# Fewer, longer weight loads, a reordered W2 and one unevenly spread load of keys in a two-layer decode kernel

## The chip, the cores and the metric

The kernel runs on one core of a Trainium2 chip. Its time is the device time of one execution in microseconds; the time shown is the median of several executions. A profile is one more execution, traced by the hardware: all durations in this document come from such traces. A core has five engines (TensorE or PE, VectorE or DVE, ScalarE or ACT, GpSimd or POOL, SyncE or SP), each with its own instruction stream, and 16 DMA engines that move data between DRAM and the core's memory of 128 partitions. SP and ACT issue the transfers here, each in its own queue; all transfers of both queues run on the same 16 DMA engines. A transfer tells by a semaphore that it has landed.

## The reference

One token goes twice through attention with a key/value cache and an MLP, with a residual around each and a normalization ahead of each:

```python
x = A_x                                            # 1 x 1 x 640
x = x + _A_ref(_layernorm(x), k_cache, v_cache, wq, wo)
x = x + _B_ref(_layernorm(x), w1, w2)
x = x + _A_ref(_layernorm(x), k_cache, v_cache, wq, wo)
x = x + _B_ref(_layernorm(x), w1, w2)
```

`_A_ref` makes 32 queries of 128 from x (wq is 640 x 4096), scores each against its head's 8192 keys, takes a softmax, sums the head's 8192 values by it, and multiplies the 32 results by wo (4096 x 640). `_B_ref` is x times w1 (640 x 1728), a ReLU, and times w2 (1728 x 640). All is float32. Keys and values are 268 MB and are needed in both layers, so nearly all of them are loaded twice.

## The kernel before

Keys and values lie in DRAM in units, one contiguous block a unit, with 128 rows, one row a partition (`UNITS`, `ORDER`, lines 41 to 82). Most units are 6 MB (48 KB a partition) and hold parts of two heads; heads 0 to 3 and 28 to 31 have smaller ones (4 MB, 2 MB and less). Units are loaded into `ring`, a tile of 133 KB a partition that a first-fit search fills (`place`, line 158). `pump` (line 177) issues the next unit's load from SP as soon as a place is free; `release` (line 231) gives a place back when PE has read it, and pumps again. Layer 0 goes through the heads from 0 to 31; layer 1 takes 31 to 24 first, of which some units are kept in the ring, and ends with 3, 2, 1, 0 (`HEADS`, line 83).

For each head PE makes the scores (`scores`, line 484, matmul at L489), DVE and ACT the softmax, PE the sum of the values (`values`, L540), and DVE and PE reduce it to a column (`output`, L557 to L581). Work that belongs to no single head runs between the pieces of a head, as chores taken in order from two lists (`due`, line 713; `work_off`, line 667; `side_work`, line 738):

- Heads are taken in eight runs of four (`HG` = 4, `NG` = 8). At the first head of a run, `run_out` (line 682) multiplies the last run's four results by wo (`projected`, L458), and then has ACT load the part of wo of the next run: `load_wo` (line 259) loads 128 x 2560 floats, 1280 KB, into `wo_t`.
- At the third head of a run, `queries_of` (line 676) makes the next run's queries from the run's part of wq (`wide_queries`, line 411, matmul at L416), and then has ACT load the part for the run after it: `load_wq` (line 254), also 128 x 2560 floats, into `wq_t`.

Each of the two tiles has a single buffer, so a load waits until PE has read what stood there. The first part of wq and of wo are loaded at the start from SP, and a run's wq at the start of layer 1 by a call of its own.

W2 lies in DRAM as 128 rows of 14 blocks of 640 floats. The blocks are loaded by SP in parts, 0 to 4 and 4 to 8 in `pump` (L199) once the last unit of a layer is issued, and 8 to 10, 10 to 12, 12 and 13 by `more_of_w2` (line 208, L210); a part takes its columns of every row, so that its rows lie 14 x 640 floats apart in DRAM. In layer 0 some of them are issued within `mlp` (line 815), after PE has read the tile that they go to.

The order of the loads in the queues is that of the program, per issuing engine. The program gives loads a semaphore out of eight in turn; a load whose semaphore is still in use waits on its issuing engine for the earlier landing.

Of the kernel before, what the change touches and what calls it, by code (L numbers as in the profile page):

```python
# [10 lines left out]
F32 = mybir.dt.float32  # L11
# [69 lines left out]
    ]  # L81
ORDER = [(h, i) for h in range(H) for i in range(len(UNITS[h]))]
HEADS = [list(range(H)), [*range(31, 23, -1), *range(12, 24), *range(4, 12), 3, 2, 1, 0]]
KEPT = [(29, 0), (29, 1), (29, 6)]
BY_WO = KEPT[0]
BESIDE = 4
# [3 lines left out]
FLAT = 3072  # L90
EDGE = 4096
BIG = 1536


def wide(kind, piece):
# [18 lines left out]


@with_exitstack
def decode_kernel(ctx: ExitStack, tc: tile.TileContext, x, kv, wq, wo, w1, w2, out):
    nc = tc.nc
    consts = ctx.enter_context(tc.tile_pool(name="consts", bufs=1))
    wts = ctx.enter_context(tc.tile_pool(name="wts", bufs=1))  # L120
# [56 lines left out]
    def pump():  # L177
        while todo:
            layer, u = todo[0]
            n = size(u)  # L180
            at = place(layer, u, n)
            if at is None:
                return
            todo.pop(0)
            o = dram_at[u]
            nc.sync.dma_start(
                ring[:, 8 * at : 8 * (at + n)],
                kv[o : o + 8 * P * n].rearrange("(p m) -> p m", p=P),
            )
            for t, (_, kind, piece) in enumerate(UNITS[u[0]][u[1]]):  # L190
                m = wide(kind, piece)
                live[layer, u, t] = at, m
                at_of[layer, u, t] = ring, 8 * at
                at += m
            if not todo or layer < todo[0][0]:
                assert all(a + m <= RING for a, m in live.values())
                live["w2"] = RING, W2_UNITS
                for a, b in W2_PARTS[:: 1 - 2 * layer]:
                    nc.sync.dma_start(w2_t[:, a:b], w2[:, a:b])  # L199
        n = (FB - SLOTS) * D // 8  # L200
        if not w2_rest:
            at = place(1, (0, None), n)
            if at is not None:
                w2_rest.append(ring[:, 8 * at : 8 * (at + n)].rearrange("p (b d) -> p b d", d=D))
                for a, b in W2_MORE:
                    more_of_w2(a, b, w2_rest[0][:, a - SLOTS : b - SLOTS])

    def more_of_w2(a, b, where):
        rows = W2_LAST if a == FB - 1 else P
        nc.sync.dma_start(where[:rows], w2[:rows, a:b])  # L210

    def load_into(u, where, queue):
        n = 8 * size(u)
# [35 lines left out]
                if (of, its) == (h, kind):  # L249
                    yield piece, (L, (owner, i), t)  # L250

    wq_t, wo_t = {}, {}

    def load_wq(g, queue):
        t = wts.tile([P, NB * HG * DH], F32, name="wq_t")
        wq_t[g] = t.rearrange("p (c n) -> p c n", c=NB)
        queue.dma_start(t, wq[P * g : P * g + P])

    def load_wo(L, g, queue):

        wo_t[g] = wts.tile([P, HG, D], F32, name="wo_t")
        first, end = (L and g == 0), HG - (not L and g == NG - 1)
        if end < HG:
            load_into(BY_WO, wo_t[g][:, end], queue)
            at_of[0, BY_WO, 0] = wo_t[g][:, end], 0
        queue.dma_start(wo_t[g][:, first:end], wo[g][:, first:end])

    def wo_of(L, h):
        return wo_last if h == H - 1 or (L and h == 0) else wo_t[h // HG][:, h % HG]

    xr = work.tile([P, DR], F32, name="xr", bufs=2)
    load_wq(0, nc.sync)
# [116 lines left out]
    def queries(g, xc, r):  # L389

        pq = ps_m.tile([P, 512], F32, name="px")
        for c in range(NB):
            for j in range(HG):
                nc.tensor.matmul(
                    pq[32 * j : 32 * j + 32, :DH],
                    xc[:, c : c + 1].to_broadcast([P, 32]),
                    wq_t[g][:, c, j * DH : (j + 1) * DH],
                    start=(c == 0),
                    stop=(c == NB - 1),
                )  # L400
        yield "dve"
        row = work.tile([P, DR], F32, name="q_row")[:, :DH]
        nc.vector.tensor_scalar(row, pq[:, :DH], r[0], SCALE, op0=ALU.mult, op1=ALU.mult)
        yield "pe"
        pt = ps_m.tile([P, 512], F32, name="px")
        nc.tensor.matmul(pt[:, :HG], row, sel[:, :HG], start=True, stop=True)
        yield "dve"
        qT[g] = work.tile([P, HG], F32, name="qT", bufs=2)
        nc.vector.tensor_copy(qT[g], pt[:, :HG])

    def wide_queries(g, xc, r):

        pq = ps_m.tile([P, 512], F32, name="px")
        for c in range(NB):
            strip = c % 4
            nc.tensor.matmul(  # L416
                pq[32 * strip : 32 * strip + 32],
                xc[:, c : c + 1].to_broadcast([P, 32]),
                wq_t[g][:, c],
                start=c < 4,  # L420
                stop=c in (1, 2, 3, 4),
                skip_group_check=True,
            )
        for j in range(HG):
            yield "dve"
            row = work.tile([P, DR], F32, name="q_row")[:, :DH]
            mine = pq[:, j * DH : (j + 1) * DH]
            nc.vector.tensor_scalar(row, mine, r[0], SCALE, op0=ALU.mult, op1=ALU.mult)  # L428
            yield "pe"
            nc.tensor.matmul(  # L430
                mine[:, :1], row, one_of_each, start=True, stop=True, skip_group_check=True
            )
        yield "dve"
        qT[g] = work.tile([P, HG], F32, name="qT", bufs=2)
        nc.vector.tensor_copy(qT[g], pq.rearrange("p (j d) -> p j d", d=DH)[:, :, 0])

    def centre_query(g, j):

        mine = wq_t[g][:, :, j * DH : (j + 1) * DH]
        pq = ps_m.tile([P, 512], F32, name="px")  # L440
        for c in range(NB):
            nc.tensor.matmul(
                pq[:, :DH],
                ones.to_broadcast([P, P]),
                mine[:, c],
                start=c == 0,
                stop=c == NB - 1,
            )
        yield "dve"
        for c in range(NB):  # L450
            nc.vector.scalar_tensor_tensor(
                mine[:, c], pq[:, :DH], -1.0 / D, mine[:, c], op0=ALU.mult, op1=ALU.add
            )
# [195 lines left out]
    def attention_and_mlp(L, xr, s, before=None):  # L649
# [1 line left out]
        heads = HEADS[L]  # L651
        last = heads[-1]
        runs = [heads[a : a + HG] for a in range(0, H, HG)]
        groups = [run[0] // HG for run in runs]
        runs[-1] = runs[-1][:-1]

        acc = ps_m.tile([P, 512], F32, name="acc")
# [17 lines left out]

        def queries_of(k):
            yield from wide_queries(groups[k], xc, r)
            yield "dve"
            if k + 1 < NG:
                load_wq(groups[k + 1], nc.scalar)  # L680

        def run_out(k):

            projected(L, acc, runs[k], o_cols[k], k == 0, False)
            yield "dve"
            load_wo(L, groups[k + 1], nc.scalar)

        def first_of_last():
            projected(L, acc, runs[-1][:2], o_cols[NG - 1], False, False)
# [125 lines left out]
    def mlp(L, o, last, xp, ph):  # L815
# [1 line left out]

        hidden(ph, o, mix, False, True)
        if L == 0:
            more_of_w2(SLOTS, 10, mix[:, : 2 * D].rearrange("p (b d) -> p b d", d=D))  # L820
        pd = ps_m.tile([P, 512], F32, name="pm")
        times_rows(pd, wo_of(L, last), o, True, True)
        in_wait(64)
# [38 lines left out]
        for b in early:  # L862
            product(b)
            for part in () if L else W2_MORE[1:]:
                if b == part[1] - 11:
                    more_of_w2(*part, w2_t[:, part[0] - 10 : part[1] - 10])

        pj = ps_m.tile([P, 512], F32, name="acc")
        for g in range(2):
# [57 lines left out]
        for c in range(NB):  # L927
            g = c % 4
            nc.tensor.matmul(
                pq[32 * g : 32 * g + 32, :DH],  # L930
                cols[:, c : c + 1].to_broadcast([P, 32]),
                wq_t[NG - 1][:, c, (HG - 1) * DH :],
                start=c < 4,
                stop=c in (1, 2, 3, 4),
                skip_group_check=True,
            )
# [40 lines left out]
def _laid_out(A_x, A_k_cache, A_v_cache, A_wq, A_wo, B_w1, B_w2):  # L977
# [5 lines left out]
    for u in ORDER:  # L983
        n = 8 * size(u)
        block = kv[o : o + P * n].reshape(P, n)
        o += P * n
        a = 0
        for h, kind, piece in UNITS[u[0]][u[1]]:
            if kind == "k":
                r, c, m = piece  # L990
                part = k[h, :, :, r, c : c + m]
            else:
                b, r, m = piece
                part = v[h, :, b, :, r : r + m]
            part = part.reshape(P, -1)
            block[:, a : a + part.shape[1]] = part
            a += part.shape[1]
    w2 = np.zeros((P, FB, D), np.asarray(B_w2).dtype)
    for b, f in enumerate(_hidden_rows()):
        w2[f >= 0, b] = np.asarray(B_w2)[f[f >= 0]][:, _COLS]  # L1000

    wq = np.asarray(A_wq).reshape(NB, P, NG, HG * DH).transpose(2, 1, 0, 3)
    return {
        "x": np.repeat(np.asarray(A_x).reshape(D)[_COLS].reshape(4, DR), 32, axis=0),
        "kv": kv,
        "wq": wq.reshape(NG * P, NB * HG * DH),
        "wo": np.asarray(A_wo)[:, _COLS].reshape(NG, HG, DH, D).transpose(0, 2, 1, 3),
        "w1": np.asarray(B_w1).reshape(NB, P, DFF).transpose(1, 0, 2),
        "w2": w2,
    }  # L1010


# [22 lines left out]
```

## Time and profile before

| what | us |
|---|---|
| median of 3 runs | 1350.23 (1348.06 to 1351.61) |
| profiled execution | 1349.67 |
| span of its trace, first to last instruction | 1347.9 |
| TensorE clock granted, mean share | 0.788 |

A page of the profile has the busy time of each engine, then the span in 40 slices, the DMA queues (packets, MB, and the time that their packets took as a share of 16 engines' span), the chain of work that ended last, the costliest groups of instructions, and the loads by line with the median time from issue to landing. A row such as `ring<-in_kv SPq ... x50, 6144.0 KB, 34.5` reads: tile written, tensor read, issuing queue, count, size of one, us to landing. A row of the table of windows reads: stretch, its length, busy time and number of instructions of PE, PE's weight load, DVE, ACT and POOL, then the granted clock, the busy share of the 16 DMA engines, and GB/s. The share counts a packet in the stretch where it begins, so that it can pass 1. A row of the chain of waits has start, duration, and what it was. L followed by a number is a line of the kernel's file.

### The profile page before, as it was taken

Reading aid. Unit: us, or ns where it says so; the run is one execution under the profiler, and the core shown is the slowest. Engines: PE = TensorE matmul, PEld = TensorE weight load, DVE = VectorE, ACT = ScalarE, POOL = GpSimd, SP = SyncE. Lnnn points to the kernel's source line nnn. Section 1 sums busy time; section 2 is a strip of 40 time slices with the busy share of each in tenths; the row PEclk is TensorE's granted clock in tenths of the full one; section 3 lists DMA queues with packets and bytes.
Section 4 is the critical chain, followed back from the end, with each engine's and each line's share of the span. In section 5 each row is a group of like instructions: output and inputs, shape, how many; then the busy total and the mean of one; then the engine's idle time right before and its main releaser. Section 6 shows DMA issues by size and latency. Waiting matters only on the chain.

```text
span 1347.9 us, 13991 instructions
## 1 busy us (share of the span) xinstructions
PE 908.3 (67%) x6094; PEld 274.0 (20%) x6094; DVE 297.4 (22%) x979; ACT 58.5 (4%) x147; POOL 2.9 (0%) x10
## 2 busy tenths in 40 slices
PE   5563776756767657676688766567666775677667
PEld 2111121211112111222143211112112121112213
DVE  2121121211212212222223222121221212212122
ACT  0000000000000000000000000000000000000000
POOL 0000000000000000000000000000000000000000
PEclk8677688888677876778898886766878678677699
DMA  9999999999999999999999999999999999999997
GB/s 398 432 427 439 427 435 434 429 429 435 433 429 425 432 437 428 428 425 420 430 379 402 434 429 434 432 425 435 436 429 432 427 434 433 432 429 432 425 427 326
DMA packets 26005, 573.05 MB, mean 425 GB/s; under 512 B 3028, under 2 KB 3160, under 8 KB 6360
## 3 DMA queue, kind: packets, MB, share of 16 engines
q1 hardware_dynamic: 21192, 530.62, 91.9%
q10 hardware_dynamic: 4752, 41.54, 7.4%
q8 instruction: 48, 0.79, 0.2%
q14 instruction: 13, 0.11, 0.0%
HBM read 572.15 MB, written 0.00 MB: 424 GB/s over the span
## 4 chain that ended last, share of the span: by engine, by line
DMA 65%; PE 28%; DVE 4%; ACT 1%; issue 1%; ACTq 0%; SPq 0%; DVEq 0%
DMA ring<-in_kv 63%; PE outs L540 11%; PE ps L489 10%; DMA ring<-in_w 2%; DVE p L561 1%; DVE h_t L501 1%; PE px L627 1%; ACT p L515 1%; PE pm L506 1%; PE pm L527 1%; PE acc L458 1%; DMA wo_t<-in_kv 1%; DVE p L522 1%; PE px L416 1%; PE pm L574 1%
## 5 line engine op out<-in xcount | busy, mean ns | idle before, releaser
L540 PE MATMUL outs<-ring,p 128*4 128x512 f32 (+2 forms) x2160 | 354.1, 783 | 173.5 <-DMA ring<-in_kv 97.6
L489 PE MATMUL ps<-ring,spread_q 128*32 128x512 f32 (+3 forms) x2088 | 330.8, 730 | 111.2 <-DMA ring<-in_kv 110.4
L501 DVE TENSOR_REDUCE h_t<-ps 128x1 f32<-128x512 f32 x64 | 44.3, 691 | 374.3 <-PE ps L489 374.2
L540 PEld LDWEIGHTS outs<-ring,p 128*4 128x4 f32 x2160 | 49.5, 95 | 346.1 <-issue 208.0
L489 PEld LDWEIGHTS ps<-ring,spread_q 128*32 128x32 f32 x2088 | 66.5, 126 | 242.5 <-issue 158.5
L515 ACT ACTIVATE p<-ps,h_t 128x512 f32<-128x512 f32 x63 | 43.3, 687 | 1173.8 <-DVE h_t L507 1173.8
L522 DVE STREAM_TRANSPOSE p<-p 128x128 f32<-128x128 f32 x256 | 79.8, 312 | 63.5 <-ACT p L515 56.9
L574 PE MATMUL pm<-ones,p 128*128 128x1 f32 (+1 forms) x128 | 25.5, 269 | 97.5 <-DVE p L561 97.5
L557 DVE TENSOR_SCALAR p<-outs,ind 128x128 f32<-128x128 f32 x64 | 22.4, 351 | 297.3 <-PE outs L540 297.3
L561 DVE SCALAR_TENSOR_TENSOR p<-outs,ind,p 128x128 f32<-128x128 f32 x188 | 66.0, 351 | 6.7
L506 PE MATMUL pm<-ident,h_t 128*128 128x128 f32 x128 | 33.0, 342 | 40.2 <-DVE h_t L501 40.1
L574 PEld LDWEIGHTS pm<-ones,p 128*128 128x128 f32 x128 | 20.1, 197 | 166.6 <-DVE p L561 164.6
L627 PE MATMUL px<-w_t,wct 128*128 128x448 f32 (+1 forms) x80 | 44.2, 637 | 0.0
L527 PEld LDWEIGHTS pm<-ind,h_t 128*128 128x128 f32 x128 | 27.0, 262 | 78.8 <-issue 78.8
L428 DVE TENSOR_SCALAR q_row<-px,ln_r 128x128 f32<-128x128 f32 x56 | 19.5, 348 | 96.4 <-PE ps L489 56.3
L506 PEld LDWEIGHTS pm<-ident,h_t 128*128 128x128 f32 x128 | 20.2, 198 | 89.7 <-DVE h_t L501 87.8
L416 PE MATMUL px<-wq_t,ln_xc 128*32 128x512 f32 x140 | 32.8, 753 | 0.0
L527 PE MATMUL pm<-ind,h_t 128*128 128x1 f32 x128 | 32.4, 323 | 0.0
L530 DVE RECIPROCAL h_t<-pm 128x1 f32<-128x1 f32 x64 | 10.8, 168 | 93.0 <-PE pm L527 93.0
L430 PEld LDWEIGHTS px<-sel,q_row 128*128 128x128 f32 x112 | 20.9, 233 | 37.7 <-DVE q_row L428 29.4
L458 PE MATMUL acc<-wo_t,o_cols 128*32 128x160 f32 x488 | 27.8, 382 | 0.0
L507 DVE TENSOR_REDUCE h_t<-pm 128x1 f32<-128x128 f32 x64 | 18.6, 291 | 35.7 <-PE pm L506 35.7
(126 smaller groups left out, 229.4 us busy)
## 6 DMA issues: line engine op xcount, KB each, us to landing
ring<-in_kv SPq DMA_DIRECT2D x50, 6144.0 KB, 34.5
ring<-in_kv SPq DMA_DIRECT2D x24, 4096.0 KB, 31.8
ring<-in_kv SPq DMA_DIRECT2D x29, 2048.0 KB, 28.8
ring<-in_kv SPq DMA_DIRECT2D x4, 5120.0 KB, 30.9
wq_t<-in_wq ACTq DMA_DIRECT2D x14, 1280.0 KB, 21.3
wo_t<-in_wo ACTq DMA_DIRECT2D x12, 1280.0 KB, 21.7
ring<-in_kv SPq DMA_DIRECT2D x9, 1024.0 KB, 24.2
ring<-in_kv SPq DMA_DIRECT2D x4, 1280.0 KB, 9.0
```

The costliest lines, as they stand in the source:

```text
L416: nc.tensor.matmul(pq[32 * strip : 32 * strip + 32], xc[:, c : c + 1].to_broadcast([P, 32]), wq_t[g][:, c], start=c < 4, stop=c in (1, 2, ...
L458: nc.tensor.matmul(acc[32 * g : 32 * g + 32, :DR], col.to_broadcast([col.shape[0], 32]), wt[:, g * DR : (g + 1) * DR], start=first, stop=last,
L489: nc.tensor.matmul(hd.ps[32 * g : 32 * g + 32, c : c + n], spread_q[:, 3 - r : 35 - r], tile_of[:, at + g * n : at + (g + 1) * n], start=f ...
L501: nc.vector.tensor_reduce(hd.nm, hd.ps, AX.X, ALU.max, negate=True)
L506: nc.tensor.matmul(pt[:, :P], hd.nm.to_broadcast([P, P]), ident, start=True, stop=True)
L515: nc.scalar.activation(hd.p, hd.ps, AF.Exp, bias=hd.low, scale=scale, accum_out=hd.l)
L522: nc.vector.transpose(hd.all_p[:, b * P : (b + 1) * P], hd.p[:, b * P : (b + 1) * P])
L527: nc.tensor.matmul(pt[:, :1], hd.l.to_broadcast([P, P]), ind[:, 4:5], start=True, stop=True)
L540: nc.tensor.matmul((hd.out if r0 < 2 else hd.out_2)[32 * g : 32 * g + 4, r0:r1].rearrange("p r d -> p (r d)"), hd.all_p[:, 32 * i : 32 * i ...
L561: nc.vector.scalar_tensor_tensor(oc, hd.out[:, r], ind[:, r : r + 1], oc, op0=ALU.mult, op1=ALU.add)
L574: nc.tensor.matmul(pt[:, :n], part, mask.to_broadcast([P, n]), start=i == 0, stop=i == len(parts) - 1,)
L627: nc.tensor.matmul(pt[:, :n], wct[:, c], w1_t[:, c, f : f + n], start=(c == 0), stop=(c == NB - 1),)
```

## The change

Three things are changed.

1. **Joint loads.** `wq_t` and `wo_t` become the two halves of one tile, `both_t`. For six of the eight runs of each layer, the wo part of the coming run and the wq part of the run after it lie side by side in a new DRAM tensor `wqo` (128 rows of 20,480 bytes) and are loaded by one transfer of 2560 KB, issued where wo's was. wq's own load at the end of `queries_of` is gone; the first wq loads and the last wo load of a layer stay as they were.
2. **W2's parts** are laid out in DRAM one after the other, each as 128 contiguous rows; the loads of `pump` and those of `more_of_w2` become one function, `part_of_w2`.
3. **A split load of keys.** In each layer one load of 2048 KB (half the keys of head 28 in layer 0, of head 1 in layer 1; 16 KB a partition) is issued as two transfers: partitions 16 to 127 as before, and partitions 0 to 15 from a copy in a new DRAM tensor `apart`, written as 2 runs of 8 rows with a gap between the runs.

```diff
+GROUPS = [[heads[a] // HG for a in range(0, H, HG)] for heads in HEADS]
...
+SPLIT = [(0, (28, 2)), (1, (1, 0))]
+FEW = 16
+GAP = 128
...
-            nc.sync.dma_start(
-                ring[:, 8 * at : 8 * (at + n)],
-                kv[o : o + 8 * P * n].rearrange("(p m) -> p m", p=P),
-            )
+            where = ring[:, 8 * at : 8 * (at + n)]
+            block = kv[o : o + 8 * P * n].rearrange("(p m) -> p m", p=P)
+            few = FEW if (layer, u) in SPLIT else 0
+            nc.sync.dma_start(where[few:], block[few:])
+            if few:
+                part = apart[SPLIT.index((layer, u))][:, :-GAP]
+                nc.sync.dma_start(where[:few], part.rearrange("k (r m) -> k r m", r=few // 2))
...
-                    nc.sync.dma_start(w2_t[:, a:b], w2[:, a:b])
+                    part_of_w2(a, b, w2_t[:, a:b])
...
-    def more_of_w2(a, b, where):
+    def part_of_w2(a, b, where):
         rows = W2_LAST if a == FB - 1 else P
-        nc.sync.dma_start(where[:rows], w2[:rows, a:b])
+        part = w2[P * D * a : P * D * b].rearrange("(p b d) -> p b d", p=P, d=D)
+        nc.sync.dma_start(where[:rows], part[:rows])
...
+    both_t = wts.tile([P, 2 * HG * D], F32, name="both_t")
+    wq_t = both_t[:, : HG * D].rearrange("p (c n) -> p c n", c=NB)
+    wo_t = both_t[:, HG * D :].rearrange("p (j d) -> p j d", d=D)
 
     def load_wq(g, queue):
-        t = wts.tile([P, NB * HG * DH], F32, name="wq_t")
-        wq_t[g] = t.rearrange("p (c n) -> p c n", c=NB)
-        queue.dma_start(t, wq[P * g : P * g + P])
+        queue.dma_start(both_t[:, : HG * D], wq[P * g : P * g + P])
 
-    def load_wo(L, g, queue):
+    def load_wo(L, k, queue):
 
-        wo_t[g] = wts.tile([P, HG, D], F32, name="wo_t")
-        first, end = (L and g == 0), HG - (not L and g == NG - 1)
+        g = GROUPS[L][k]
+        if 0 < k < NG - 1:
+            queue.dma_start(both_t, wqo[L, k - 1])
+            return
+        first, end = (L and k == NG - 1), HG - (not L and k == NG - 1)
...
     def queries_of(k):
         yield from wide_queries(groups[k], xc, r)
-        yield "dve"
-        if k + 1 < NG:
-            load_wq(groups[k + 1], nc.scalar)
 
     def run_out(k):
 
         projected(L, acc, runs[k], o_cols[k], k == 0, False)
         yield "dve"
-        load_wo(L, groups[k + 1], nc.scalar)
+        load_wo(L, k + 1, nc.scalar)
...
+    apart = np.zeros((len(SPLIT), 2, 4 * FEW * size(SPLIT[0][1]) + GAP), k.dtype)
+    for i, (_, u) in enumerate(SPLIT):
+        o = 8 * P * sum(size(v) for v in ORDER[: ORDER.index(u)])
+        apart[i, :, :-GAP] = kv[o : o + 8 * FEW * size(u)].reshape(2, -1)
...
+    wqo = [
+        [np.concatenate([wq[b], wo[a].reshape(P, HG * D)], 1) for a, b in zip(gs[1:-1], gs[2:])]
+        for gs in GROUPS
+    ]
...
-        "w2": w2,
+        "wqo": np.array(wqo),
+        "w2": np.concatenate([w2[:, a:b].reshape(-1) for a, b in W2_PARTS + W2_MORE]),
+        "apart": apart,
```

More of the change, by code (lines that the diff above doesn't have):

```diff
@@ L116, in decode_kernel @@
 @with_exitstack
-def decode_kernel(ctx: ExitStack, tc: tile.TileContext, x, kv, wq, wo, w1, w2, out):
+def decode_kernel(ctx: ExitStack, tc: tile.TileContext, x, kv, wq, wo, wqo, w1, w2, apart, out):
     nc = tc.nc
@@ L205, in pump @@
                 for a, b in W2_MORE:
-                    more_of_w2(a, b, w2_rest[0][:, a - SLOTS : b - SLOTS])
-    def more_of_w2(a, b, where):
+                    part_of_w2(a, b, w2_rest[0][:, a - SLOTS : b - SLOTS])
+    def part_of_w2(a, b, where):
         rows = W2_LAST if a == FB - 1 else P
-        nc.sync.dma_start(where[:rows], w2[:rows, a:b])
+        part = w2[P * D * a : P * D * b].rearrange("(p b d) -> p b d", p=P, d=D)
+        nc.sync.dma_start(where[:rows], part[:rows])
     def load_into(u, where, queue):
@@ L250, in pieces_of @@
                     yield piece, (L, (owner, i), t)
-    wq_t, wo_t = {}, {}
+    both_t = wts.tile([P, 2 * HG * D], F32, name="both_t")
+    wq_t = both_t[:, : HG * D].rearrange("p (c n) -> p c n", c=NB)
+    wo_t = both_t[:, HG * D :].rearrange("p (j d) -> p j d", d=D)
     def load_wq(g, queue):
-        t = wts.tile([P, NB * HG * DH], F32, name="wq_t")
-        wq_t[g] = t.rearrange("p (c n) -> p c n", c=NB)
-        queue.dma_start(t, wq[P * g : P * g + P])
-    def load_wo(L, g, queue):
-        wo_t[g] = wts.tile([P, HG, D], F32, name="wo_t")
-        first, end = (L and g == 0), HG - (not L and g == NG - 1)
+        queue.dma_start(both_t[:, : HG * D], wq[P * g : P * g + P])
[5 more added lines that the diff above has]
+        first, end = (L and k == NG - 1), HG - (not L and k == NG - 1)
         if end < HG:
-            load_into(BY_WO, wo_t[g][:, end], queue)
-            at_of[0, BY_WO, 0] = wo_t[g][:, end], 0
-        queue.dma_start(wo_t[g][:, first:end], wo[g][:, first:end])
+            load_into(BY_WO, wo_t[:, end], queue)
+            at_of[0, BY_WO, 0] = wo_t[:, end], 0
+        queue.dma_start(wo_t[:, first:end], wo[g][:, first:end])
     def wo_of(L, h):
-        return wo_last if h == H - 1 or (L and h == 0) else wo_t[h // HG][:, h % HG]
+        return wo_last if h == H - 1 or (L and h == 0) else wo_t[:, h % HG]
     xr = work.tile([P, DR], F32, name="xr", bufs=2)
@@ L396, in queries @@
                     xc[:, c : c + 1].to_broadcast([P, 32]),
-                    wq_t[g][:, c, j * DH : (j + 1) * DH],
+                    wq_t[:, c, j * DH : (j + 1) * DH],
                     start=(c == 0),
@@ L418, in wide_queries @@
                 xc[:, c : c + 1].to_broadcast([P, 32]),
-                wq_t[g][:, c],
+                wq_t[:, c],
                 start=c < 4,
@@ L437, in centre_query @@
     def centre_query(g, j):
-        mine = wq_t[g][:, :, j * DH : (j + 1) * DH]
+        mine = wq_t[:, :, j * DH : (j + 1) * DH]
         pq = ps_m.tile([P, 512], F32, name="px")
@@ L653, in attention_and_mlp @@
         runs = [heads[a : a + HG] for a in range(0, H, HG)]
-        groups = [run[0] // HG for run in runs]
+        groups = GROUPS[L]
         runs[-1] = runs[-1][:-1]
@@ L819, in mlp @@
         if L == 0:
-            more_of_w2(SLOTS, 10, mix[:, : 2 * D].rearrange("p (b d) -> p b d", d=D))
+            part_of_w2(SLOTS, 10, mix[:, : 2 * D].rearrange("p (b d) -> p b d", d=D))
         pd = ps_m.tile([P, 512], F32, name="pm")
@@ L865, in mlp @@
                 if b == part[1] - 11:
-                    more_of_w2(*part, w2_t[:, part[0] - 10 : part[1] - 10])
+                    part_of_w2(*part, w2_t[:, part[0] - 10 : part[1] - 10])
         pj = ps_m.tile([P, 512], F32, name="acc")
@@ L931, in mlp @@
                 cols[:, c : c + 1].to_broadcast([P, 32]),
-                wq_t[NG - 1][:, c, (HG - 1) * DH :],
+                wq_t[:, c, (HG - 1) * DH :],
                 start=c < 4,
@@ L1000, in _laid_out @@
         w2[f >= 0, b] = np.asarray(B_w2)[f[f >= 0]][:, _COLS]
-    wq = np.asarray(A_wq).reshape(NB, P, NG, HG * DH).transpose(2, 1, 0, 3)
+    wq = np.asarray(A_wq).reshape(NB, P, NG, HG * DH).transpose(2, 1, 0, 3).reshape(NG, P, HG * D)
+    wo = np.asarray(A_wo)[:, _COLS].reshape(NG, HG, DH, D).transpose(0, 2, 1, 3)
+    wqo = [
+        [np.concatenate([wq[b], wo[a].reshape(P, HG * D)], 1) for a, b in zip(gs[1:-1], gs[2:])]
+        for gs in GROUPS
+    ]
     return {
@@ L1005, in _laid_out @@
         "kv": kv,
-        "wq": wq.reshape(NG * P, NB * HG * DH),
-        "wo": np.asarray(A_wo)[:, _COLS].reshape(NG, HG, DH, D).transpose(0, 2, 1, 3),
+        "wq": wq.reshape(NG * P, HG * D),
+        "wo": wo,
+        "wqo": np.array(wqo),
         "w1": np.asarray(B_w1).reshape(NB, P, DFF).transpose(1, 0, 2),
-        "w2": w2,
+        "w2": np.concatenate([w2[:, a:b].reshape(-1) for a, b in W2_PARTS + W2_MORE]),
+        "apart": apart,
     }
```

## The prediction, made before the changed kernel ran

> **What bounds the kernel now.** I read the page's head and its DMA part first, then the chain that ended last, then the table of windows over the whole run.
>
> ```profile
> span 1347.9 us, 13991 instructions
> DMA packets 26005, 573.05 MB, mean 425 GB/s; under 512 B 3028, under 2 KB 3160, under 8 KB 6360
> q1 hardware_dynamic: 21192, 530.62, 91.9%
> q10 hardware_dynamic: 4752, 41.54, 7.4%
> q8 instruction: 48, 0.79, 0.2%
> q14 instruction: 13, 0.11, 0.0%
> DMA 65%; PE 28%; DVE 4%; ACT 1%; issue 1%; ACTq 0%; SPq 0%; DVEq 0%
> ```
>
> The two loading queues (q1 is SP's, q10 is ACT's: its 41.54 MB are the weights) fill 91.9 + 7.4 = 99.3% of the time of 16 engines. The chain is 65% transfer. So the time is the time in which 16 DMA engines move 573 MB, and an edit counts only where it shortens the engines' work or one of the few stretches in which engines stand still. The windows tell where those are (their last two columns are the DMA share and GB/s):
>
> ```profile
> 0.00:10.00 10.00, 2.28 (x26) 2.14 (x30) 2.78 (x22) 0.00 (x0) 0.82 (x7) 1.00 0.82 323
> 100.00:200.00 100.00, 60.91 (x364) 17.27 (x356) 19.38 (x59) 4.49 (x11) 0.00 (x0) 0.74 1.00 431
> 690.00:730.00 40.00, 33.63 (x376) 16.16 (x370) 12.13 (x51) 2.38 (x7) 1.10 (x2) 0.90 0.95 368
> 1100.00:1200.00 100.00, 70.58 (x427) 20.90 (x428) 20.40 (x65) 4.40 (x11) 0.00 (x0) 0.76 1.00 431
> 1300.00:1336.00 36.00, 27.18 (x278) 10.54 (x281) 8.35 (x28) 1.93 (x5) 0.00 (x0) 1.00 1.00 422
> 1336.00:1347.90 11.90, 7.82 (x148) 5.25 (x140) 2.70 (x14) 0.37 (x2) 0.55 (x1) 0.95 0.40 154
> ```
>
> Only the start (10 x 0.18 = 1.8 us), the change of layers at 690 to 730 (40 x 0.05 = 2.0 us) and the end (11.9 x 0.60 = 7.1 us) have idle engines. The end, microsecond by microsecond:
>
> ```profile
> 1337.00:1338.00 1.00, 0.94 (x8) 0.78 (x7) 0.56 (x5) 0.37 (x2) 0.00 (x0) 1.00 0.91 330
> 1338.00:1339.00 1.00, 0.97 (x29) 0.88 (x32) 0.20 (x2) 0.00 (x0) 0.00 (x0) 1.00 0.64 246
> 1339.00:1340.00 1.00, 1.00 (x23) 0.70 (x16) 0.20 (x2) 0.00 (x0) 0.00 (x0) 1.00 0.63 256
> 1340.00:1341.00 1.00, 1.00 (x33) 0.93 (x32) 0.81 (x5) 0.00 (x0) 0.00 (x0) 1.00 0.56 230
> 1341.00:1342.00 1.00, 1.00 (x29) 0.71 (x18) 0.16 (x1) 0.00 (x0) 0.06 (x1) 1.00 0.55 220
> 1342.00:1343.00 1.00, 0.65 (x21) 0.37 (x16) 0.00 (x0) 0.00 (x0) 0.49 (x1) 1.00 0.38 114
> 1343.00:1344.00 1.00, 0.52 (x16) 0.20 (x12) 0.00 (x0) 0.00 (x0) 0.00 (x0) 1.00 0.06 15
> ```
>
> 16 x (1 - share) is the number of engines already done: 1.4, then 5.8, 5.9, 7.0, 7.2, 9.9 and 15.0. So some six engines finish by about 1338.5 and the other half only between 1341.5 and 1343.5, though each load gives every engine the same rows. The same stands ahead of the change of layers:
>
> ```profile
> 690.00:691.00 1.00, 0.59 (x20) 0.29 (x10) 0.70 (x2) 0.33 (x1) 0.00 (x0) 1.00 0.95 399
> 691.00:692.00 1.00, 0.88 (x6) 0.74 (x6) 0.00 (x0) 0.04 (x1) 0.00 (x0) 1.00 0.61 256
> 692.00:693.00 1.00, 0.71 (x8) 0.29 (x12) 0.22 (x1) 0.00 (x0) 0.00 (x0) 1.00 0.58 231
> ```
>
> Again 16 x 0.39 to 16 x 0.42, six or seven engines, are done some 4 us ahead of the rest (the next load is issued only at 693). The likely cause is in the first fence: the 48 instruction fetches take 0.2% of 16 x 1347.9 us, so near 0.9 us each, and one fetch is one packet on one engine; 24 a layer on half of the engines are 3 x 0.9 = 2.7 us, most of that lead. The trace doesn't number the engines.
>
> **Joint loads of wq and wo.** 12 pairs of 1280 KB loads become 12 loads of 2560 KB: six a layer. The bytes stay. What goes is packets:
>
> ```profile
> ring<-in_kv SPq DMA_DIRECT2D x50, 6144.0 KB, 34.5
> wq_t<-in_wq ACTq DMA_DIRECT2D x14, 1280.0 KB, 21.3
> wo_t<-in_wo ACTq DMA_DIRECT2D x12, 1280.0 KB, 21.7
> ```
>
> q1's 21192 packets are its 148 loads into the chip at 128 rows and 16 small completions each (146 x 144 + 2 x 80 for the two loads of 64 rows, + 8 for the output), so a row is one packet even at 48 KB, and a row of 20 KB will be one too. What a packet costs beside its bytes follows from the two queue rows: q10 takes 0.074 x 16 x 1347.9 / 4752 = 336 ns for 8742 B, q1 0.919 x 16 x 1347.9 / 21192 = 935 ns for 25038 B; the line through both is 27.2 B/ns and 14 ns a packet (12 to 17 by the rounding of 7.4%). A pair made joint saves 144 packets: 144 x 14 / 16 = 0.13 us an engine, and 12 of them **1.5 us** (1.3 to 1.8). It is all on the path, since the engines are never idle there.
>
> What moves: wq of the next run used to be asked for right after the queries that used the old one; now it waits for the projection at the start of the next run, where wo is asked for, and two heads later the queries need it. The nearest places in the chain of waits are these (L458 is the projection, L416 the queries):
>
> ```profile
> 457.77 1.91 PE acc L458 x32
> 500.45 2.52 PE px L416 x9
> 770.90 1.09 PE acc L458 x32
> 803.27 1.72 PE px L416 x9
> ```
>
> That leaves 42.7 us, and 32.4 us at the tightest, for the landing. wo alone lands in 21.7 us as 8 rows an engine; the joint load has 8 rows too. If the two queues take turns by packet, each row is longer by 10 KB / 27.2 = 0.38 us, 3 us in all: 25 us. If landing goes with the bytes it is 2 x 21.7 = 43 us, 11 us late. I take 25: shared by bytes, 1.31 MB beside as much of q1 would have landed in 2 x 1.31 / 431 = 6 us, while 8 turns of a 48 KB row and a 10 KB row are 8 x (1.82 + 0.39) = 17.7 us, far nearer to 21.7. Were it late, PE would stand for 11 us with all that follows on it (scores, ring release, SP's next issues), but SP has 34.5 us of issued work ahead: the engines would go on, and it still costs nothing. Without that cover it would cost 11 us once, at 803. On ACT, the joint load waits for the same projection that wo's did, ahead of the same exponential; one wait and one issue a run less. SP is past nothing new. Cost of the move: 0.
>
> **W2 contiguous.** Same loads, rows and packets; only the distance of rows in DRAM changes. Small packets show whether the old distance costs: at 1340 to 1341 all packets are W2's of 5 and 2.5 KB, and a busy engine moves 230 / 0.56 / 16 = 25.7 B/ns; a 5 KB packet at 27.2 B/ns and 14 ns should give 25.3. Nothing is left for the stride: **0**. Above, the windows 1300 to 1336 and 690 to 730 bound the gain: (431 - 422) / 431 x 36 = 0.8 us, and at the change of layers (0.95 x 431 - 368) / 431 x 40 = 3.9 us for everything there that is slow while busy, of which W2 is one load of several. So 0 to 2 us; I take 0, by the nearest row. A loss has no place: contiguous rows are what all key and value loads have.
>
> **The split load.** One 2048 KB load a layer: 128 rows of 16 KB, 8 rows an engine, 2.1 MB / 431 GB/s = 4.9 us. After: 112 rows are 7 an engine (4.3 us), and 16 rows on two engines are 8 each (4.9 us). 14 engines save 4.9 / 8 = **0.6 us**; two have 7 more rows, **4.3 us** more. If the two are of the six that end 4 to 5 us early, the last engine is 0.6 us earlier, at 690 and at the end: 2 x 0.6 = **1.2 us**. A smaller lead gives less: at 4.5 us the gain is 0.2. That the small load stays on two engines I take from its source, written as 2 runs of 8 rows, and from the one transfer of before that is not 16 deep: the output's 4 rows count 4 completions in q1's sum, not 16. At 690 the gain is on the path:
>
> ```profile
> 649.01 35.88 DMA ring<-in_kv
> 696.40 6.46 DMA ring<-in_w
> 1328.26 15.55 DMA ring<-in_w
> ```
>
> PE's end of layer 0 follows a landing, and the W2 parts behind it and the last ones at 1343.8 are waited for by PE. SP has two issues more. One issue takes a third of a microsecond (this one is ACT's):
>
> ```profile
> 772.05 0.34 ACTq L266 DMA_DIRECT2D wo_t<-in_wo  x1
> ```
>
> Later loads of that queue are issued 0.34 us later; the 34.5 us of issued work hide it: 0, and 0.7 us without that cover. [...]
>
> **Sum.** 1.5 + 0 + 1.2 = 2.7 us off the profiled execution's 1349.67 (span 1347.9 and 1.8 around it): 1347.0. That execution lies 0.56 us below the median of the runs, 1350.23; off the median it is **1347.5**, 0.2% faster. A change under 0.3% (4.05 us: below 1346.18 or above 1354.28) can hardly be told from none in this kernel, whose three runs spread from 1348.06 to 1351.61.
>
> **Rivals.** A, slower: the two engines are late ones. Nothing in the trace numbers them, and 9 or 10 of 16 finish in the late half. A layer loses as soon as one of the pair leads the last engine by less than 4.3 us, and the whole change is slower than before when the lead is under 4.3 - 1.5 / 2 = 3.55 us. If one of the pair is a last one, both layers end 4.3 us later: + 8.6 - 1.5 = 7.1 us, **1357.3**. Against: the early group is large, and its lead fits the 4.3 us.
>
> B, the split doesn't do what it says: the 16 rows go over all engines, one each. Then every engine has its 8 rows again, 1.2 us are missing and 2 x 16 more small packets cost nothing: **1348.7**. [...]
>
> C, faster by more. What SP waits for, before it issues:
>
> ```profile
> SPq L186 <- DMA wq_t<-in_wq: 13.9, 2, 7.8
> SPq L210 <- PE acc L640: 22.7, 1, 22.7
> ```
>
> The stride of W2 does cost, 2 us, and SP's two waits for wq vanish with its loads, so that the 2.0 us idle at the change of layers shrink by one: 2.7 + 3 = 5.7 us, **1344.5**. For it: 368 GB/s at a share of 0.95; against: the packets at 1340, and that SP's long wait at the change of layers, L210, is for PE.
>
> D, the joint load comes late and the cover fails: + 11 - 2.7: **1358.5**. Against: a share of 1.00 in every window between.
>
> **How the numbers follow.** Forecast 0.52, A 0.16, B 0.12, C 0.17, D 0.03. Of the forecast, the runs' own spread puts about 0.07 below 1346.18; a little of A is a pair in the middle, near 1352 and within 0.3%. Faster 0.25, same 0.58, slower 0.17. The range leaves out the lower tail of C (0.05) and the body of A and D (0.14): 1344.0 to 1354.5; the forecast's own range, by its terms' bounds and the runs' spread, is 1346 to 1349.
>
> **What would show it.** Right: q10 with 4752 - 1728 = 3024 packets at the same bytes; two loads of 1792 KB and two of 256 KB; shares in the last microseconds with six engines no longer done early, but four; the last W2 landing 2 to 3 us earlier in the span; PE's L416 not waiting for a DMA. Wrong: one or two engines busy alone for 4 us at 690 and at the end (A); shares as before (B); PE L416 waiting for the joint tile (D). What would make it wrong above all is which two engines the small load runs on.

## The result, and the profile after

The changed kernel takes 1372.55 us (median of 4 runs, 1369.2 to 1373.07) against 1349.2 us before in the same comparison: ratio 1.0164, 95% interval 1.0151 to 1.0177. It is slower by 23.4 us by the medians, by 22 by the ratio, where 2.7 us faster was forecast. The head and the queues on the page of the changed kernel:

```profile
span 1371.3 us, 13974 instructions
q1 hardware_dynamic: 21196, 530.62, 91.9%
q10 hardware_dynamic: 3024, 41.53, 7.2%
both_t<-in_wqo ACTq DMA_DIRECT2D x12, 2560.0 KB, 24.8
```

The packets are those that were forecast, 3024 on ACT's queue, and so is the joint load's landing (24.8 us; 25 was forecast). The two queues still fill 91.9 + 7.2 = 99.1% of 16 engines' time, yet the span is 23.4 us longer, so the same bytes took busy engines longer. Added up packet by packet from the two traces, SP's queue took 1260.8 us of each engine, where it took 1238.9 before: 22 us more. The engines were idle for 8.6 us on average, 5.9 before. The table of windows says where (last columns: DMA share, GB/s). First some of the run's longer stretches:

```profile
500.00:600.00 100.00, 69.45 (x429) 19.83 (x432) 23.62 (x76) 3.89 (x10) 0.00 (x0) 0.76 1.00 431
600.00:680.00 80.00, 49.32 (x370) 15.77 (x362) 15.70 (x52) 3.11 (x8) 0.00 (x0) 0.77 1.00 368
1100.00:1200.00 100.00, 70.25 (x426) 19.95 (x426) 20.95 (x68) 3.96 (x11) 0.00 (x0) 0.74 1.00 432
1300.00:1336.00 36.00, 18.80 (x112) 5.46 (x112) 6.36 (x21) 1.56 (x4) 0.00 (x0) 0.76 0.99 302
```

and then five microseconds at a time around the split load of layer 0, which SP issued at 587:

```profile
600.00:605.00 5.00, 4.17 (x30) 1.39 (x22) 0.69 (x1) 0.00 (x0) 0.00 (x0) 0.78 0.94 403
605.00:610.00 5.00, 1.93 (x16) 0.76 (x19) 1.55 (x6) 0.78 (x2) 0.00 (x0) 0.91 1.04 344
610.00:615.00 5.00, 3.90 (x24) 0.53 (x16) 1.18 (x5) 0.00 (x0) 0.00 (x0) 0.75 1.06 220
615.00:620.00 5.00, 4.46 (x60) 2.84 (x60) 1.32 (x7) 0.00 (x0) 0.00 (x0) 1.00 1.03 200
620.00:625.00 5.00, 0.31 (x4) 0.00 (x0) 0.43 (x3) 0.00 (x0) 0.00 (x0) 0.77 0.94 170
625.00:630.00 5.00, 0.55 (x4) 0.20 (x8) 0.00 (x0) 0.00 (x0) 0.00 (x0) 0.50 0.95 307
630.00:635.00 5.00, 3.57 (x18) 0.69 (x10) 0.98 (x2) 0.18 (x1) 0.00 (x0) 0.71 1.00 420
```

In the same place the kernel before moved 419 and 415 GB/s:

```profile
600.00:620.00 20.00, 14.47 (x120) 5.50 (x116) 4.31 (x15) 0.78 (x2) 0.00 (x0) 0.85 0.99 419
620.00:640.00 20.00, 12.86 (x118) 3.38 (x110) 4.95 (x18) 0.78 (x2) 0.00 (x0) 0.83 1.01 415
```

For 25 us the engines are busy and move little more than half of what they otherwise do. Against 431 GB/s the five slow rows lack (87 + 211 + 231 + 261 + 124) x 5 = 4570 KB, 10.6 us of the stream. The same stretch in layer 1, 1295 to 1320 (377, 213, 184, 180 and 239 GB/s), lacks 962 x 5 = 4810 KB, 11.2 us. Together 21.8 us (21 against what the kernel before moved in the same stretches): nearly all of the loss is in these two stretches, and both lie some 20 us behind the issue of a split load, at 587 and 1282.

The move of wq costs nothing, as forecast. The queries' matmul by its line: nothing with DMA in its name among what its engine waited for.

```profile
L427 PE MATMUL px<-both_t,ln_xc x140: 591/592/1061, 64.9 to 1240.0; 128*32 128x512 f32 x140
its engine sat idle before it (us, times) until:
  issue: 24.2, 54
```

### The profile page after: what moved, and what is told of

The parts are those of the page before. It is cut to its first block, busy times and chain, and to the rows that moved or that the text cites. A ratio compares the mean times of both kernels' runs of the same rounds, so it can differ in the third digit from the quotient of the medians.

```text
span 1371.3 us, 13974 instructions
## 1 busy us (share of the span) xinstructions
PE 899.1 (66%) x6094; PEld 272.3 (20%) x6094; DVE 297.2 (22%) x979; ACT 58.5 (4%) x147; POOL 2.9 (0%) x10
## 3 DMA queue, kind: packets, MB, share of 16 engines
q1 hardware_dynamic: 21196, 530.62, 91.9%
q10 hardware_dynamic: 3024, 41.53, 7.2%
## 4 chain that ended last, share of the span: by engine, by line
DMA 67%; PE 26%; DVE 4%; ACT 1%; issue 1%; SPq 0%; ACTq 0%; DVEq 0%
DMA ring<-in_kv 62%; PE ps L500 10%; PE outs L551 10%; DMA ring<-in_apart 3%; DMA ring<-in_w 2%; PE px L638 1%; DVE p L572 1%; PE px L427 1%; ACT p L526 1%; DVE h_t L512 1%; PE pm L517 1%; PE pm L538 1%; PE pm L585 1%; PE px L441 1%; DVE p L533 0%
## 5 line engine op out<-in xcount | busy, mean ns | idle before, releaser
L551 PE MATMUL outs<-ring,p 128*4 128x512 f32 (+2 forms) x2160 | 344.0, 761 | 185.6 <-DMA ring<-in_kv 114.0
L427 PE MATMUL px<-both_t,ln_xc 128*32 128x512 f32 x140 | 33.9, 773 | 0.0
L469 PE MATMUL acc<-both_t,o_cols 128*32 128x160 f32 x488 | 26.4, 366 | 0.0
## 6 DMA issues: line engine op xcount, KB each, us to landing
both_t<-in_wqo ACTq DMA_DIRECT2D x12, 2560.0 KB, 24.8
```

The source lines that it names most:

```text
L427: nc.tensor.matmul(pq[32 * strip : 32 * strip + 32], xc[:, c : c + 1].to_broadcast([P, 32]), wq_t[:, c], start=c < 4, stop=c in (1, 2, 3, ...
L551: nc.tensor.matmul((hd.out if r0 < 2 else hd.out_2)[32 * g : 32 * g + 4, r0:r1].rearrange("p r d -> p (r d)"), hd.all_p[:, 32 * i : 32 * i ...
```

## The experiments

Two things in the split load are new: a load of 112 partitions on all engines, and a load of 16 partitions on two (q1 counts 2 completions for each, 16 for a whole load). The theories were P (the 112: where its rows land), T (the two engines), J (the joint loads), and R (the number of rows an engine, or their place in DRAM).

**e1_no_split.** The uneven loads are issued whole.

```diff
-            few = FEW if (layer, u) in SPLIT else 0
+            few = 0
```

> The changed kernel with both uneven loads issued whole again (128 partitions in one transfer); the joint loads and the contiguous W2 stay. Theory P (the 112-partition load gives each engine 7 rows, so that engines write partitions that others write in every other load, and transfers slow each other while both kinds are under way) and theory T (the 2-engine load of 16 partitions slows all): the 23 us loss is gone and the 1.5 us of the prediction's first term are left, 1347.7 us, ratio 0.9985 to 1.000. Theory J (the joint loads lose the time): still 1372 us, ratio 1.017.

Measured: 1349.86 us, ratio 1.0007 (0.9998 to 1.0016). The loss is the split load's, and J falls. The 1.5 us of gain doesn't show here: the ratio lies just outside the 0.9985 to 1.000 that was expected.

**e2_split_alone.** The kernel before with the `SPLIT` lines of the diff and no other.

> The kernel before with the split load alone. P and T: the whole loss and the 1.5 us of the joint loads on top, 1372 to 1375 us, ratio 1.017 to 1.019, with two stretches of some 25 us at 300 GB/s, one a layer. J: 1349 us, ratio 1.00.

Measured: 1372.23 us, ratio 1.0171 (1.0157 to 1.0185). The split load makes the whole loss by itself.

**e3_16_on_all.** The small load goes over 16 engines, one row each (alone, in row six of m1 below, such loads keep 16 x 0.96 = 15.4 engines busy).

```diff
-                part = apart[SPLIT.index((layer, u))][:, :-GAP]
-                nc.sync.dma_start(where[:few], part.rearrange("k (r m) -> k r m", r=few // 2))
+                nc.sync.dma_start(where[:few], block[:few])
```

> The changed kernel, its 16 partitions loaded from the plain cache by a transfer of 16 rows, one an engine, in place of the 2-engine load; the 112 stay as they are. P: the loss stays, 1365 to 1375 us, ratio 1.012 to 1.019, since the 112-partition load stays. T: the loss is gone, 1348 us, ratio 0.999.

Measured: 1368.24 us, ratio 1.0146 (1.013 to 1.0162). Most of the loss stays without any 2-engine load: T falls as the main cause. The 16 rows are still a load of their own to 16 neighbouring partitions, which is slow too (row six of m1 below), so e3 doesn't say how the loss divides between them and the 112.

**e4_columns.** The same bytes for two engines, but an eighth of each row; the main load has 128 partitions again.

```diff
+            cut = 8 * n * (P - few) // P
-            nc.sync.dma_start(where[few:], block[few:])
+            nc.sync.dma_start(where[:, :cut], block[:, :cut])
...
-                nc.sync.dma_start(where[:few], part.rearrange("k (r m) -> k r m", r=few // 2))
+                nc.sync.dma_start(where[:, cut:], part.rearrange("k (r m) -> k r m", r=P // 2))
...
```

> The changed kernel with the same bytes given to two engines, but as the last eighth of each of the 128 partitions' columns (64 rows of 2 KB an engine); the main load has all 128 partitions and 14 KB of each. P: the main load's engines write their usual partitions again, only two engines write elsewhere for some 5 us: within 1346 to 1351 us, ratio 0.997 to 1.002. T: the loss stays, 1365 to 1375 us, ratio 1.012 to 1.019.

Measured: 1353.82 us, ratio 1.0033 (1.002 to 1.0046), 3 us over P's range. With all partitions in the main load most of the loss is gone. What is left is again a busy, slower stretch at the load of each layer:

```profile
600.00:620.00 20.00, 14.70 (x135) 5.39 (x130) 5.17 (x18) 0.78 (x2) 0.00 (x0) 0.92 0.99 373
1280.00:1300.00 20.00, 14.59 (x96) 3.60 (x88) 5.32 (x17) 0.78 (x2) 0.00 (x0) 0.85 1.00 388
```

(431 - 373) x 20 and (431 - 388) x 20 are 2.0 MB, 4.7 us (3.8 against the 419 and 422 GB/s of the kernel before in the same stretches). The main load, 14 KB of each of 128 rows, is at full speed alone (row ten of m1 below), so the two engines that write 64 partitions each (taken as two from the form of the source, which gave 2 completions in the changed kernel) are what is left as the cause. A 2-engine load on such partitions isn't free either; only its price is smaller.

**e5_joint_alone, e6_w2_alone.** The other two parts of the change, each by itself on the kernel before.

> The kernel before with the joint loads alone. The first term of the prediction: 1.5 us less, 1347.8 us, ratio 0.9985 to 0.9995, if what e1 gave back was W2's part. If the packets' saving is given back at the change of layers: ratio 1.000 to 1.001, with q10's time down by 1.6 us an engine and as much more idle time.

> The kernel before with W2's parts contiguous alone. By the prediction 0 us: ratio 0.9995 to 1.0005. If it is W2's new place that took the joint loads' 1.5 us in e1: ratio 1.001 to 1.002.

Measured: the joint loads 1348.42 us against 1348.96, ratio 0.9990 (0.9982 to 0.9999); W2 1348.68 us, ratio 0.9998 (0.9989 to 1.0007). In the profile of the first, ACT's queue takes

```profile
q10 hardware_dynamic: 3024, 41.53, 7.3%
```

0.1 points less than before, 1.3 us an engine by these rounded figures; added up packet by packet it took 98.0 us of each engine, where it took 99.6 before, 1.6 us less. The joint loads alone are the only version whose interval lies below 1, and only just: 0.1 to 2.4 us faster, 1.35 in the middle. That e1, which has both parts, came out at 1.0007 overlaps with it only at its edge (0.9998), so that a small loss of the two together isn't excluded.

**m1_loads_alone.** Loads without any computation, one kind a stretch, in a single execution:

```python
slots = ring.rearrange("p (s m) -> p s m", s=8)          # rows of 4096 floats, 16 KB
...
block = kv[o : o + P * M].rearrange("(p m) -> p m", p=P)
where = slots[:, i % SLOTS]
nc.sync.dma_start(where[rows], block[rows])              # rows: 0:128, 16:128, 0:64, 32:96:4, ...
```

> Loads alone: all computation is left out, and the output is a piece of the cache. Ten stretches of 24 loads of rows of 16 KB into eight slots, one kind a stretch, with a wait between: 128 partitions; 16 to 127; 0 to 111; 0 to 63; 32 to 95; 0 to 15; 16 partitions from 32 to 92 in steps of 4; 128 alternating with 112 and the 2-engine load; 128 alternating with 112 and 16 rows on all; 128 with 14 KB of each row. [...] Theory R (the number of rows an engine, or the place in DRAM, is the cause): 0 to 63 and 32 to 95 alike, and 0 to 15 like the steps of 4; 112 alone slow whatever the partitions.

The windows, one row a stretch in the order of that list (here the columns are DVE, POOL, clock, DMA share, GB/s):

```profile
0.70:121.10 120.40, 0.00 (x0) 0.00 (x0) 1.00 0.99 418
121.30:287.90 166.60, 0.06 (x2) 0.00 (x0) 1.00 0.99 264
288.10:460.00 171.90, 0.04 (x1) 0.00 (x0) 1.00 0.99 256
460.20:584.80 124.60, 0.01 (x1) 0.00 (x0) 1.00 0.99 202
585.00:646.50 61.50, 0.00 (x0) 0.00 (x0) 1.00 0.97 409
646.70:706.30 59.60, 0.01 (x1) 0.00 (x0) 1.00 0.96 106
706.50:725.90 19.40, 0.00 (x0) 0.00 (x0) 1.00 0.85 324
726.10:968.40 242.30, 0.01 (x1) 0.00 (x0) 1.00 0.74 208
968.60:1163.00 194.40, 0.00 (x0) 0.00 (x0) 1.00 0.97 259
1163.20:1269.20 106.00, 0.03 (x2) 0.00 (x0) 1.00 0.99 416
```

Rows four and five are the same load but for its partitions: 0 to 63 get 202 GB/s, 32 to 95 get 409, with the engines as busy. Rows six and seven are 16 rows, one an engine: next to each other 106 GB/s, four apart 324 and idle for part of the time. Row ten, 14 KB of each of 128 rows, is at full speed, so the bytes an engine have no part in it. The 112 partitions get 264 and 256. In row eight, 12 whole loads with 12 pairs of 112 and 2-engine loads take 242.3 us where 24 whole ones take 120.4: 10.2 us more for each pair. A split load costs as much in the kernel, but that is partly chance. Near the end of row eight

```profile
930.00:960.00 30.00, 0.00 (x0) 0.00 (x0) 1.00 0.15 57
```

only 16 x 0.15 = 2.4 engines are at work: it seems that the extra rows of all 12 pairs pile up on the same two engines, which the kernel's one split load a layer cannot do. In row nine, with the 16 rows on all engines, the price is 6.2 us, where e3 lost 9.5 for each of its split loads; what makes up the rest in the kernel isn't shown. Row nine does show that loads slow each other: one after another its parts would take 12 x (5.0 + 6.9 + 2.5) = 173 us by rows one, two and six, and it took 194.4.

**m2_same_bytes_elsewhere.** What was left for R: the 112 rows' number or their place in DRAM. Here the same block goes to other partitions.

```python
part = kv[o + (8 - n) * 16 * M : o + P * M].rearrange("(e m) -> e m", e=16)   # n = 7: the same 112 rows
nc.sync.dma_start(where[rows, : n * M], part)                                # rows: 32:96:4 or 0:16
```

> Loads alone again, all computation left out, with rows of 4 KB and 96 loads a stretch, six places in turn. Stretch 1: 128 partitions. 2: 112 rows to partitions 16 to 127, 7 rows an engine. 3: the same 112 rows of the same DRAM block, 7 an engine, to 16 partitions from 32 to 92 in steps of 4. 4: the same again to partitions 0 to 15. 5 and 6: 64 rows to 0 to 63 and to 32 to 95. 7: all 128 rows, 8 an engine, to the 16 partitions in steps of 4. Theory P: only where the rows land matters: stretch 3 near stretch 1 (over 380 GB/s), stretch 2 near 264 as with long rows, stretch 4 near 106, 5 near 200, 6 and 7 near stretch 1. Theory R (7 rows an engine, or their place in DRAM): stretch 3 and 4 like stretch 2, near 264.

```profile
52.10:178.20 126.10, 0.00 (x0) 0.00 (x0) 1.00 1.00 399
178.40:337.70 159.30, 0.01 (x1) 0.00 (x0) 1.00 1.01 276
337.90:443.90 106.00, 0.00 (x0) 0.00 (x0) 1.00 0.98 416
444.10:850.50 406.40, 0.00 (x0) 0.00 (x0) 1.00 1.00 108
850.70:974.20 123.50, 0.01 (x1) 0.00 (x0) 1.00 1.01 204
974.40:1051.40 77.00, 0.00 (x0) 0.00 (x0) 1.00 0.92 327
1051.60:1172.50 120.90, 0.01 (x1) 0.00 (x0) 1.00 0.98 416
```

This too is a single execution. Rows two to four are the same 112 rows of a block in DRAM, 7 an engine: 276 GB/s to partitions 16 to 127, 416 to 16 partitions four apart, 108 to 16 neighbours. R falls; the partitions decide. (Row six, the short loads to 32 to 95, was expected near row one's 399 and got 327. Its engines are idle for 8% of the time, which is not all of the distance; the rest isn't explained.)

**e7_split_while_in_step.** Does a split load cost more late in a layer? The changed kernel with the split moved to near each layer's start.

```diff
-SPLIT = [(0, (28, 2)), (1, (1, 0))]
+SPLIT = [(0, (1, 0)), (1, (28, 2))]
```

> The changed kernel with its split loads moved to where the engines are still nearly in step: head 1's first half of keys in layer 0, head 28's in layer 1, both near the layer's start. If the price is that of the 112-partition load and the 2-engine load by themselves (10.4 us a pair when they alternate with whole loads in m1), 2 x 10 us: ratio 1.014 to 1.016. If a good part of it comes from the 5 us that the engines are apart late in a layer, which make each engine run beside others that are at another load for longer: 2 x 5 to 2 x 8 us, ratio 1.006 to 1.011.

Measured: 1363.39 us, ratio 1.011 (1.0093 to 1.0126), the upper edge of what was expected if the engines' distance matters. The slow stretches are shorter:

```profile
30.00:50.00 20.00, 4.84 (x38) 1.27 (x34) 1.62 (x5) 0.00 (x0) 0.00 (x0) 0.66 1.00 364
720.00:760.00 40.00, 31.21 (x302) 11.77 (x306) 13.93 (x48) 2.43 (x6) 0.00 (x0) 0.91 1.02 358
```

(431 - 364) x 20 = 1.3 MB and (431 - 358) x 40 = 2.9 MB, 3.1 and 6.8 us, in place of 10.6 and 11.2. These 9.9 us are not all of the 14.7 that this run lost: added up packet by packet, its engines were also idle for 10.4 us, 5.9 before. The shorter stretches agree with the engines' lead making them longer, but other loads are neighbours here too, so it is not shown that nothing else differs.

## Why the prediction was wrong, point by point

- **What bounds the kernel**: right. The stream of 16 engines (99.3% of their time taken before, 99.1% after) sets the time in both, and the loss is time of the stream.
- **Joint loads, 1.5 us and no cost of the move**: right in mechanism (packets as counted, landing 24.8 us), and the runs agree with the size: the queue's packets took 1.6 us less, and alone the loads gained 0.1 to 2.4 us. Together with W2 (e1) no gain showed. Two readings were a little off, without effect: counted from the issue at 772.05, the tightest time for the landing was 31.2 us and not 32.4, and the rounding of 7.4% puts a packet's cost at 11 to 18 ns, not 12 to 17.
- **W2, 0 us**: right, 0.9998 alone.
- **The split load, "14 engines save 4.9 / 8 = 0.6 us; two have 7 more rows, 4.3 us more"**: this step failed, and its error is nearly the whole result: 10.6 and 11.2 us lost where 0.6 each was to be gained. It took a row's 0.6 us as the engine's own, wherever the row lands. But 0.6 us is the price in a load of 128 partitions. In the stretch from 605 to 630 the 16 KB rows took 617 ns on average before and 1155 after, by the packets of the traces; from 1295 to 1320, 616 and 1257. The 8 KB rows there, which are all of whole loads, went from 313 to 454 ns in the first stretch: the loads beside the split one were slowed too. Taken alone, the 112 partitions move 1.83 MB at 264 GB/s in 6.9 us, where 4.3 us were reckoned. In m2 112 rows move at 276 GB/s to these partitions and at 416 to 16 partitions four apart. So in these runs the partitions set a row's price; how the 112 come to lose that much stays open.

  No run shows the 1.2 us of this term, that a row moved to another engine takes its 0.6 us off the load: what the runs showed in its place is 21.8 us lost in the two stretches, and 1368.24 us (e3) and 1353.82 (e4) with the load cut in two other ways.
- **Rival A, the pair are late ones**: it had the sign, and not the mechanism. The windows speak against it: with the small load on all engines (e3) some seven engines are done 4 us early, as before, and the loss is there all the same. With it on two (the changed kernel) four to seven are done early, and one to three work on alone for some 2 us. Ends of e3, then of the changed kernel:

```profile
1357.00:1358.00 1.00, 1.00 (x26) 0.86 (x22) 0.34 (x3) 0.00 (x0) 0.00 (x0) 1.00 0.56 223
1359.00:1360.00 1.00, 1.00 (x22) 0.70 (x18) 0.16 (x1) 0.00 (x0) 0.29 (x1) 1.00 0.55 198
1360.00:1361.00 1.00, 0.58 (x20) 0.42 (x16) 0.00 (x0) 0.00 (x0) 0.26 (x1) 1.00 0.18 64
1361.00:1362.00 1.00, 0.95 (x24) 0.31 (x16) 0.00 (x0) 0.00 (x0) 0.00 (x0) 1.00 0.01 3
```

```profile
1359.00:1360.00 1.00, 1.00 (x18) 0.52 (x10) 0.36 (x2) 0.00 (x0) 0.00 (x0) 1.00 0.63 206
1361.00:1362.00 1.00, 0.97 (x29) 0.85 (x32) 0.23 (x2) 0.00 (x0) 0.00 (x0) 1.00 0.72 297
1363.00:1364.00 1.00, 1.00 (x30) 0.94 (x33) 0.84 (x5) 0.00 (x0) 0.00 (x0) 1.00 0.54 192
1364.00:1365.00 1.00, 1.00 (x28) 0.71 (x18) 0.16 (x1) 0.00 (x0) 0.03 (x1) 1.00 0.18 59
1365.00:1366.00 1.00, 0.31 (x12) 0.00 (x0) 0.00 (x0) 0.00 (x0) 0.52 (x1) 1.00 0.15 47
1366.00:1367.00 1.00, 0.65 (x16) 0.42 (x16) 0.00 (x0) 0.00 (x0) 0.00 (x0) 1.00 0.06 23
```

  16 x 0.44 = 7 engines are done in the first; in the second 16 x 0.37 = 5.9, then 16 x 0.28 = 4.5, and near the end 16 x 0.15 = 2.4 engines go on. The pair seems to have been among the early ones and to have used up its lead and more; since no row numbers the engines, that stays an inference, as does the laying of the lead to instruction fetches, which no run tested. Some of the 4.3 us between e3 and the changed kernel may be a cost of A's kind.
- **Rival B** (the small load on all engines, 1348.7): the small load did run on two engines, as q1's count tells: 4 packets more, that is 2 for each split load, and 112 + 16 + 16 + 2 is 146 where a whole load has 144. And where e3 made it run on all, the time was 1368 us.
- **Rivals C and D**: neither. W2's stride costs nothing that shows, the queries wait for no load, the share at the change of layers didn't rise (0.92 from 690 to 730, 0.95 before), and SP's two waits for wq stayed (11.3 us in all, 13.9 before).

The range ended at 1354.5, and the dearest rival at 1358.5, because every case took a row's price as fixed. The signs to look for named idle engines and lone engines, and none a busy engine with fewer GB/s, which is what came.

## What to carry to other kernels

In these runs a load's price depended on which partitions it wrote. Alone and with rows of 16 KB, 128 partitions and 32 to 95 took over 400 GB/s here, 0 to 63 and 112 partitions 202 to 264, and 16 neighbours 106: a part of the partitions can cost more time than the whole (24 loads of 112 took 166.6 us, 24 of 128 took 120.4). Before cutting a load by partitions, time that very set of partitions alone and beside the loads that it will run with. When the DMA share stays at 1 and GB/s falls, as from 610 to 625 here (0.94 to 1.06 at 170 to 220 GB/s), look at where the bytes go, not at when they were issued.

## What the runs showed of the hardware that was not expected

- 16 neighbouring partitions take loads at 106 to 108 GB/s, 16 partitions four apart (32 to 92) at 324 in m1 and 416 in m2; in m2 the bytes are the same and the DMA share is 1.00 for the neighbours, 0.98 for the others.
- 0 to 63 take 202 to 204 GB/s, 32 to 95 409.
- 112 partitions get 256 to 276 GB/s, less than the 7/8 x 431 = 377 that they would have if they took as long as all 128. In what order the engines take these rows was not seen, and why they lose that much stays open.
- A slow load slows the others beside it: whole loads that alternate with loads of 112 and of 16 partitions take 194.4 us in m1, where the parts one after another come to 173; in the changed kernel the 8 KB rows of whole loads took 454 ns beside a split load, 313 before; and two engines that write 64 partitions each beside a whole load cost some 4 us in e4.
